# A gated linear attention with an SSM block on one core: weights converted by bit moves, transposes taken to VectorE, and the SSM block moved one group closer

## The chip, the cores and the metric

One core of a Trainium2 chip. The time is device microseconds of one execution, the median of a kernel's executions. Each kernel was run together with runs of the kernel before on the same chip. A ratio is the mean time of one kernel's fast runs over that of the other's fast runs of the same rounds, with a 95% interval, so it is not quite the ratio of the medians quoted. Spans are from one profiled execution; a timed run lies about 2 us above its span.

Engines: PE is TensorE's matmul, PEld its weight load, DVE VectorE, ACT ScalarE, POOL GpSimd, SP SyncE; a q after a name (SPq, ACTq) is the sequencer that issues transfers. "L330" is a line of the kernel of that run, and the kernels before and after number their lines differently.

## The reference, cut to what matters

```python
# q, k, v, alpha: (4, 8, 768, 48) fp32; alpha in 0.8..1.0
for t in range(S):
    state = alpha[:, :, t, :, None] * state + einsum('bhd,bhe->bhde', k[:, :, t], v[:, :, t])
    y[:, :, t] = einsum('bhd,bhde->bhe', q[:, :, t], state)
x = y.transpose(0, 2, 1, 3).reshape(4, 768, 384)
proj = x @ w_in                       # w_in: (384, 1024), float64 numbers in memory
val, gate = proj[..., :512], proj[..., 512:]
h = a * h + val                       # step by step, a = exp(A_log)
out = (silu(gate) * h) @ w_out        # w_out: (512, 384), float64
```

The weights arrive as float64, and the kernel computes in float32. It reads each number as two 32-bit words and builds a float32 of them.

## The kernel before: the parts that the change and the argument touch

The 4 x 768 steps are handled in 12 groups of 256 (`N` = 12, `NG` = 3 groups a batch). `front(n)` turns alpha, q and k of a group, so that channels lie on partitions (TensorE transposes, tile `tp`), makes the running products `V` and `P` of alpha on DVE, scales q and k by them, computes the scores `sc` and turns k back (`tpk`). `back(n)` makes the states `z` and their sums `S_n`, the values `y`, and turns the features (`tpx` to `xT`). `ssm(n)` is the projection `pj`, the scan `hh`, the gate `sg` and the output `o`. All are generators; the order of their steps is written by hand.

```python
        def split_unit(u):                       # a unit: 128 x 384 weights, 12 of them
            lo, hi = words[u][..., 0], words[u][..., 1]
            dst = units[u][0]
            nc.scalar.activation(lo.bitcast(FP32), lo, AF.Copy, scale=2.0 ** -52)
            # ... DVE: ex = hi & 0x7FF00000 ; dst = hi & 0xFFFFF | 0x41000000
            nc.scalar.activation(ex.bitcast(FP32), ex, AF.Relu, scale=-8.0, bias=bias[:, 3:4])
            nc.scalar.activation(ex, ex.bitcast(FP32), AF.Relu, scale=-1.0, bias=bias[:, 4:5])
            nc.scalar.activation(dst, dst, AF.Copy, bias=-7.0)
        # join_unit: DVE ex = sign | ex ; GpSimd dst += lo ; GpSimd dst *= ex

        # in front(n), for alpha, q and k
            def turned(name, jj):
                tp = ps_tp.tile([C, 2, GC], FP32, tag="tp", name="tp")
                for u in range(2):
                    j = 2 * jj + u
                    for c in range(G):
                        nc.tensor.transpose(tp[:, u, ds(c * C, C)], pad[name][:, c, 2 * j:2 * j + 2, :], ident)
                return tp
            # ... V, P: DVE scans over turned("a"); Q = turned("q") * P; K = turned("k") * V

        # in back(n)
            for x in range(GR):                  # sums of the states of blocks of 64 steps
                # ... nc.vector.tensor_add(dst, S_n[:, x], src)
        # ...
            nc.sync.dma_start(out=out[b, ds(g * GC + c * C, C), :], in_=o_sb)     # in ssm(n)

        with tc.manual_schedule():
            for n in range(N + 3):
                # iteration n: front(n), back(n - 1), the projection of n - 2, the output of n - 3
```

## Time and profile before

| | before |
|---|---|
| time, median | 346.38 us (346.02 to 346.68, 3 runs) |
| span of the profiled execution | 344.2 us |
| PE busy, and idle | 309.7 us, 34.5 us |
| PE without a hole from | about 75 us on |
| period of one group after that | 24.73 us |

The prediction below shows the slices, the chain and the windows. What it takes from the groups of instructions is here: one of the three sets of input transposes, and one of the four ACT passes over a unit of weights. The columns after the count are total busy time, mean ns of one, and idle time ahead with what ended it.

```profile
L295 PE MATMUL tp<-ident,k_pad 128*128 128x128 f32 x96 | 14.4, 298 | 0.2 <-issue 0.2
...
L242 ACT ACTIVATE ex<-ex,bias 128x384 uint32<-128x384 f32 x12 | 7.4, 616 | 0.4
```

Each ACT pass has twelve instances, all in the first stage. The `tp` lines come three times (alpha, q, k), 96 matmuls each, spread over the whole run.

### The profile page before, as it was taken

Reading aid. Unit: us, or ns where it says so; the run is one execution under the profiler, and the core shown is the slowest. Engines: PE = TensorE matmul, PEld = TensorE weight load, DVE = VectorE, ACT = ScalarE, POOL = GpSimd, SP = SyncE. Lnnn points to the kernel's source line nnn. Section 1 sums busy time; section 2 is a strip of 40 time slices with the busy share of each in tenths; the row PEclk is TensorE's granted clock in tenths of the full one; section 3 lists DMA queues with packets and bytes.
Section 4 is the critical chain, followed back from the end, with each engine's and each line's share of the span. In section 5 each row is a group of like instructions: output and inputs, shape, how many; then the busy total and the mean of one; then the engine's idle time right before and its main releaser. Section 6 shows DMA issues by size and latency. Waiting matters only on the chain.

```text
span 344.2 us, 9637 instructions
## 1 busy us (share of the span) xinstructions
PE 309.7 (90%) x4233; PEld 249.6 (73%) x4233; DVE 198.6 (58%) x374; ACT 126.5 (37%) x267; POOL 32.3 (9%) x54
## 2 busy tenths in 40 slices
PE   2556696879999999999999999999999999997994
PEld 1345585757877878868868878878878878776772
DVE  2869797683566566475484494484475574314140
ACT  1356876743324324324333342333233233222111
POOL 4023652440000000000000000000000000000000
PEclk9996798989999999999999999999999999999998
DMA  9999998504704907608609409519110010010101
GB/s 129 216 218 256 238 199 125 94 2 103 130 2 97 135 2 130 104 0 146 88 1 160 73 2 170 62 38 170 29 46 4 0 48 2 2 49 0 50 0 54
DMA packets 107650, 29.02 MB, mean 84 GB/s; under 512 B 100944, under 2 KB 107088, under 8 KB 107600
## 3 DMA queue, kind: packets, MB, share of 16 engines
q1 hardware_dynamic: 104992, 27.93, 46.4%
q10 hardware_dynamic: 2608, 0.40, 1.0%
q8 instruction: 35, 0.57, 0.7%
q14 instruction: 15, 0.12, 0.1%
HBM read 23.60 MB, written 4.72 MB: 82 GB/s over the span
## 4 chain that ended last, share of the span: by engine, by line
PE 80%; DVE 8%; ACT 5%; DMA 3%; issue 2%; SPq 1%; ACTq 0%; DVEq 0%
PE pj L93 36%; PE o L107 18%; PE tp L295 9%; PE z L131 3%; PE sc L332 3%; PE y L146 3%; PE y L164 3%; PE tpk L119 3%; PE tpx L173 2%; DVE V L302 2%; DVE P L307 2%; DMA a_pad<-in_alpha_dram 2%; DMA v_sb<-in_v_dram 1%; ACT ex L242 1%; ACT ex L241 1%
## 5 line engine op out<-in xcount | busy, mean ns | idle before, releaser
L93 PE MATMUL pj<-xT,w_in 128*128 128x256 f32 x576 | 135.2, 386 | 2.9 <-ACT sg L101 2.9
L93 PEld LDWEIGHTS pj<-xT,w_in 128*128 128x128 f32 x576 | 107.1, 192 | 17.5 <-POOL w_out L250 3.0
L107 PE MATMUL o<-w_out,f 128*128 128x384 f32 x192 | 65.9, 496 | 0.1
L96 DVE TENSOR_TENSOR_SCAN hh<-a_dec,hh,pj 128x256 f32<-128x256 f32 x32 | 23.9, 747 | 69.0 <-PE pj L93 69.0
L101 ACT ACTIVATE sg<-pj 128x256 f32<-128x256 f32 x48 | 18.4, 383 | 114.1 <-DVE hh L96 114.0
L107 PEld LDWEIGHTS o<-w_out,f 128*128 128x128 f32 x192 | 35.9, 192 | 23.7 <-DVE f L102 0.7
L102 DVE TENSOR_TENSOR f<-sg,hh 128x256 f32<-128x256 f32 x48 | 20.9, 436 | 25.4 <-ACT sg L101 25.4
L302 DVE TENSOR_TENSOR_SCAN V<-tp,bias 128x256 f32<-128x256 f32 x48 | 30.1, 669 | 6.9 <-PE tp L295 6.9
L307 DVE TENSOR_TENSOR_SCAN P<-tp,iV,bias 128x256 f32<-128x256 f32 x48 | 33.4, 737 | 0.8
L312 ACT ACTIVATE junk<-V,bias 128x1024 f32<-128x1024 f32 x12 | 13.8, 1148 | 47.2 <-DVE V L302 47.2
L295 PE MATMUL tp<-ident,a_pad 128*128 128x128 f32 x96 | 13.9, 289 | 14.0 <-POOL k_pad L201 4.9
L96 DVE TENSOR_TENSOR_SCAN hh<-a_dec,pj 128x256 f32<-128x256 f32 x16 | 11.0, 685 | 23.8 <-PE pj L93 23.8
L295 PEld LDWEIGHTS tp<-ident,a_pad 128*128 128x128 f32 x96 | 11.6, 147 | 15.9 <-POOL k_pad L201 4.9
L349 POOL TENSOR_TENSOR S_n<-S_end,V 128x192 f32<-128x192 f32 x7 | 3.6, 513 | 203.5 <-DVE S_end L358 203.5
L295 PE MATMUL tp<-ident,q_pad 128*128 128x128 f32 x96 | 14.4, 292 | 8.0 <-DVE P L307 6.4
L295 PEld LDWEIGHTS tp<-ident,q_pad 128*128 128x128 f32 x96 | 11.9, 151 | 12.2 <-issue 8.6
L335 DVE COPY_PREDICATED A<-mask,sc 128x512 f32<-128x512 uint8 x24 | 16.0, 720 | 3.0 <-PE sc L332 3.0
L319 DVE TENSOR_TENSOR Q<-tp,P 128x512 f32<-128x512 f32 x24 | 15.4, 681 | 2.9 <-PE tp L295 2.9
L332 PEld LDWEIGHTS sc<-Q,K 64*64 64x64 f32 x768 | 13.7, 143 | 4.0 <-issue 3.0
L110 ACT ACTIVATE o_sb<-o 128x384 f32<-128x384 f32 x24 | 10.7, 479 | 15.5 <-PE o L107 15.5
L323 DVE TENSOR_TENSOR K<-tp,V 128x512 f32<-128x512 f32 x24 | 15.5, 681 | 0.5 <-PE tp L295 0.5
L332 PE MATMUL sc<-Q,K 64*64 64x64 f32 x768 | 15.5, 231 | 0.1
(61 smaller groups left out, 313.8 us busy)
## 6 DMA issues: line engine op xcount, KB each, us to landing
a_pad<-in_alpha_dram SPq DMA_DIRECT2D x24, 192.0 KB, 4.7
k_pad<-in_k_dram SPq DMA_DIRECT2D x24, 192.0 KB, 5.2
v_sb<-in_v_dram SPq DMA_DIRECT2D x24, 192.0 KB, 5.1
out_dram<-o_sb SPq DMA_DIRECT2D x24, 192.0 KB, 2.2
q_pad<-in_q_dram SPq DMA_DIRECT2D x22, 192.0 KB, 4.9
bits<-in_moe_w_in_dram SPq DMA_DIRECT2D x8, 384.0 KB, 5.3
bits<-in_moe_w_out_dram SPq DMA_DIRECT2D x4, 384.0 KB, 5.1
q_pad<-in_q_dram ACTq DMA_DIRECT2D x2, 192.0 KB, 5.5
```

The costliest lines, as they stand in the source:

```text
L93: nc.tensor.matmul(pj[:, i, :], w_in[:, kk, i, ds(cc * C, C)], xT[:, kk, :], start=(kk == 0), stop=(kk == NK - 1))
L96: nc.vector.tensor_tensor_scan(out=hh, data0=a_dec[:, cc:cc + 1].to_broadcast([C, GC]), data1=pj[:, 0, :], initial=prev_h[cc][:, GC - 1:GC ...
L101: nc.scalar.activation(sg, pj[:, 1, :], AF.Silu)
L102: nc.vector.tensor_mul(f[:, cc, :], sg, hh)
L107: nc.tensor.matmul(o, f[:, cc, ds(c * C, C)], w_out[:, cc, :], start=(cc == 0), stop=(cc == NI - 1))
L295: nc.tensor.transpose(tp[:, u, ds(c * C, C)], pad[name][:, c, 2 * j:2 * j + 2, :], ident)
L302: nc.vector.tensor_tensor_scan(out=V[:, 2 * jj + u, GC - 1::-1], data0=tp[:, u, ::-1], data1=bias[:, 1:2].to_broadcast([C, GC]), initial=1 ...
L307: nc.vector.tensor_tensor_scan(out=P[:, 2 * jj + u, :], data0=tp[:, u, :], data1=bias[:, 1:2].to_broadcast([C, GC]), initial=iV0[:, 2 * jj ...
L319: nc.vector.tensor_mul(Q[:, js], turned("q", jj), P[:, js])
L323: nc.vector.tensor_mul(K[:, js], turned("k", jj), V[:, js, 1:GC + 1])
L332: nc.tensor.matmul(scv[ds(R * r, R), i, c * NP + j, :], K[rows, j, steps], Q[rows, j, steps], start=True, stop=True, skip_group_check=True)
L335: nc.vector.copy_predicated(out=A[:, i].rearrange("p x t -> p (x t)"), mask=mask[:, ds(i * GP * R, GP * R)], data=sc[:, i])
```

## The change

By its title it converts the weights by bit moves and one integer add, with a range check and a complete fallback, and brings the SSM block of group n - 1 beside group n. The diff holds a third part: from group 4 on, alpha, q and k are loaded in squares of 32 x 32 and turned by VectorE. The diff, cut to its core:

```diff
+        def convert_unit(u):
+            nc.scalar.activation(lo.bitcast(FP32), lo, AF.Copy, scale=2.0 ** -29, bias=2.0 ** 23)
+            nc.scalar.activation(lo, lo.bitcast(FP32), AF.Copy, bias=-2.0 ** 23)
+            nc.vector.tensor_scalar(out=dst, in0=hi, scalar1=0x07FFFFFF, scalar2=3,
+                                    op0=ALU.bitwise_and, op1=ALU.logical_shift_left)
+            nc.vector.scalar_tensor_tensor(out=dst, in0=hi, scalar=0xC0000000, in1=dst,
+                                           op0=ALU.bitwise_and, op1=ALU.bitwise_or)
+            nc.gpsimd.tensor_add(units[u][0].bitcast(I32), units[u][0].bitcast(I32), lo.bitcast(I32))
+        def check_units(p):                       # range of three units' high words, in place
+            nc.scalar.activation(h, h, AF.Square, scale=2.0 ** -16, accum_out=left_w[:, p, 0:1])
+            nc.scalar.activation(h, h, AF.Relu, scale=-2.0 ** 60, bias=bias[:, 0:1], accum_out=left_w[:, p, 1:2])
-        (split_unit, join_unit)
...
+        staging = big.tile([C, len(units), NK * C * 2], U32, tag="big0", name="staging")   # raw weights
+        BY_VECTOR = NG + 1
+        def load_batch(b):
+            t = big.tile([C, 3, NP * NW * W], FP32, tag=f"big{1 - b % 2}", name="batch")   # b = 1: big0
+            for m, (name, src) in enumerate((("a", alpha), ("q", q), ("k", k))):
+                w0 = max(0, BY_VECTOR - NG * b) * GC // W
+                ...                               # 2 memsets on GpSimd
+                for j, nj in [(0, NP)] if w0 == 0 else [(j, 1) for j in range(NP)]:
+                    for i in range(2):
+                        for half in range(2):
+                            nc.sync.dma_start(...)      # squares: rows of 128 and of 64 bytes
+            def squares(name, dst):
+                nc.vector.transpose(dst, batches[b, name][:, :, ds(g * GC, GC)])
...
-            nc.sync.dma_start(out=out[b, ds(g * GC + c * C, C), :], in_=o_sb)
+            nc.scalar.dma_start(out=out[b, ds(g * GC + c * C, C), :], in_=o_sb)
+        def load_last(n):
+            if n == 2:
+                load_batch(1)
+            if 2 <= n < N - 2:
+                load(n + 2, "v", nc.scalar)
...
+        # F, A: a step of front(n), front(n + 1); B: back(n); P, H: projection of n - 1; O: output of n - 2
+        # C: product check; U: convert a unit; W: check three units; L, M: loads
+        early = ["FFFFLUFUFABBABB", "UUFPUUFHPUHFFPUHBBCPHABUAUBL", "FPUFHPUHFFPHBBCAPHBWAWOBWAWOM"]
+        usual = "FLPHPHFFOABBCPHABPHBAOM"
+        ending = ["PHPHOPHPHO", "OO"]
```

Queries, keys, `Kn`, `A` and the features have one buffer less than before.

## The prediction

> **What bounds the kernel now.** I read the slices of the span first, then the chain that ended last in order of time, then the table of windows, and last the groups by line and shape. The page says which engine is full, and from when:
>
> ```profile
> PE 309.7 (90%) x4233; PEld 249.6 (73%) x4233; DVE 198.6 (58%) x374; ACT 126.5 (37%) x267; POOL 32.3 (9%) x54
> ...
> PE   2556696879999999999999999999999999997994
> ...
> DVE  2869797683566566475484494484475574314140
> ...
> PEclk9996798989999999999999999999999999999998
> DMA  9999998504704907608609409519110010010101
> ```
>
> PE has holes in the first nine slices (to about 75 us) and none after. There are two stages with different limits. In the second, the chain is TensorE alone; here is most of one period, one group of 256 steps:
>
> ```profile
> 246.69 0.87 PE tp L295 x8
> 247.56 1.08 PE z L131 x64
> 248.64 5.36 PE o L107 x16
> 254.00 0.87 PE tp L295 x8
> ...
> 258.74 0.87 PE tp L295 x8
> ...
> 263.46 1.09 PE sc L332 x64
> 264.55 0.81 PE tpx L173 x6
> 265.36 2.59 PE pj L93 x12
> 267.95 0.87 PE tpk L119 x8
> ```
>
> The next period starts at 271.42, so a group takes 24.73 us: three sets of input transposes (tp) 2.61, score, state, value and turning work (sc, tpk, z, two y, tpx) 6.00, projections (pj) 10.77, output (o) 5.36. In the first stage the table of windows shows DVE as the fullest engine:
>
> ```profile
> 40.00:50.00 10.00, 7.96 (x103) 6.90 (x103) 9.30 (x19) 7.73 (x17) 6.28 (x6) 1.00 1.20 252
> 50.00:62.00 12.00, 8.73 (x148) 7.22 (x149) 9.36 (x21) 9.25 (x18) 3.74 (x4) 0.86 0.84 112
> 62.00:75.00 13.00, 9.51 (x191) 7.92 (x183) 9.59 (x19) 7.35 (x16) 6.01 (x7) 0.91 0.36 63
> ...
> 150.00:200.00 50.00, 50.00 (x703) 40.69 (x702) 30.30 (x56) 16.51 (x36) 0.51 (x1) 1.00 0.50 81
> ```
>
> (Columns: PE, weight loads, DVE, ACT, POOL, clock, DMA share, GB/s.) Between 20 and 75 us DVE is busy 45 of 55 us, 82%; ACT, with four passes for each piece of weights, is next. In the steady stage DVE uses 0.61 of its time.
>
> **What the Trainium skill says.** The title of the change hides its largest part: from group 4 on, alpha, q and k are no longer turned by TensorE but by VectorE in squares of 32, from tiles that the DMA fills in squares.
> - "VectorE: DVE Perf Modes", The three transpose paths: the VectorE transpose works on 32x32 blocks only and lands in SBUF. "Vector Engine (DVE) Microarchitecture Reference", 3.8: it sustains one element per cycle per lane. At the 0.96 GHz of these pages 1024 elements are 1.07 us; with the start-up of the ops here (a 512-wide multiply takes 681 ns, of which 533 are elements) my estimate is 1.2 us. The kernel before has no such instruction, so its trace can't confirm it.
> - "DMA: Bandwidth & Descriptors", Why small descriptors are slow (HBM only): each packet has a fixed cost beside its bytes. The trace agrees: in the packet records the median of a 192-byte packet is 15 ns, of 1024 bytes 49 ns, which is 7 ns fixed and 0.041 ns a byte.
> - "TensorE: Matmul & The Clock Gate", What's actually happening: after an idle window of about 3.4 us the clock halves. The trace agrees: the granted clock is 0.57 in the window 30 to 40, where PE waited.
>
> **The change part by part.**
> 1. *Input transposes.* 12 groups x 3 sets become 4 x 3; 24 sets x 0.87 us = 20.9 us leave TensorE in the stage where it sets the end. The period falls to 24.73 - 2.61 = 22.12.
> 2. *VectorE takes them.* 24 x 1.2 = 29 us more. A steady group on DVE before is 0.607 x 24.73 = 15.0 us; with 3.6 more it is 18.6 of 22.12 us, 84%, plus four waits of 0.5 us between a scan and its gated product (25.4 us over 48 in the table of waits). It fits with about 1.5 us to spare, so I count nothing, but it is close.
> 3. *Weights.* On ACT a piece falls from 556+611+616+507 = 2290 ns to two passes, about 1.1 us: 12 x 1.2 = 14 us less. DVE falls from three passes (427, 542, 641) to two (542, 641): 12 x 0.43 = 5 us less. POOL loses one pass of 1.0 us in 12. All in the first stage. The range check is new: 4 x 2 ACT passes over 1152 elements, estimated from the 1024-wide 1148 ns plus a 187 ns accumulator read as 1.4 us each: 11 us at the end of iteration 2.
> 4. *Schedule.* The SSM block of n - 1 stands beside group n, one iteration less behind. By the end of iteration 2 the new program has issued the projections of groups 0 and 1 and the output of 0 and is ready for the projection of group 2. I time that point by DVE. Work that stands ahead of the last state sum of group 2: conversion 12 x 1.18 minus a little for the contiguous w_out = 13.5; three groups of scans, Q, K, mask 3 x 10.1 = 30.4; states 4.2; eight gate pairs less one 8.0: 56 us. Start at 8.2 (first scan). With ACT relieved I take a busy share of 0.87 in place of 0.82: 8.2 + 64 = 72.5. From there the values 1.1, the ACT copy 1.4, two check units 5.5 that stand ahead in ACT's order, the output copy 0.5, the turned features 1.0: the projection of group 2 starts at 82.
> 5. *What TensorE has left then:* ten projections 107.7, eleven outputs 59.0, nine groups x 6.00 = 54.0: 220.7 us.
> 6. *A new wait.* The first square tile reuses the buffer of the raw weights, so its load can't start before the last check, at about 82 + 5.5 = 87.5. Each row of 192 bytes now moves as one packet of 128 and one of 64 bytes: twice the packets. By the size fit plus the 6.6 ns by which the 192-byte mean exceeds its median they take 19 and 16 ns, 1.1 ns a packet over 16 engines. Alpha of groups 4 and 5 is 8192 packets, 9 us; with two memsets of about 1.8 us ahead (estimated from 308 ns for 256 elements) and 2 us of landing it is there at about 101. DVE reaches it after about 8 us of iteration 3, waits some 5 us, and the state sums of group 3 stand behind it in DVE's order. TensorE reaches the values that need these at 82 + 9.5 and gets them at 87.5 + 19.5 - a loss near 10; I take 9, plus 2 for a cold clock after it.
> 7. *End.* The last outputs stand behind other matmuls, so the two waits for gates (about 2 us each in the chain at 316 and 334) are hidden; they are not in the sum of 5, and I add none. From the last matmul to the end 4.7 us as before (339.5 to 344.2).
>
> Sum: 82 + 220.7 + 11 + 4.7 = 318.4 us of span; the timed runs lie 2 us over the span (346.4 against 344.2): 320. As the hand-made order of the first stage is likely better than my share of 0.87, I put 318.
>
> **Rivals.**
> - *DMA becomes the bound* from iteration 3 to 6. Groups 4 to 8 need 24.6 + 36.9 thousand packets plus three loads of v, in about 75 us. At 1.1 ns that is 75 us, just enough; at the 1.25 ns that a burst of 8192 192-byte packets shows (10.2 us) it loses 10 to 15 more: 330. DMA share 0.50 with half as many packets speaks for it. ACT also issues outputs and v loads now, and waits for DMA slots that square loads hold.
> - *VectorE becomes the bound.* If a square transpose takes 2.2 us, DVE needs 23.7 us a group and the period is about 25: no gain in the steady stage, 335 to 340. One element a cycle speaks against it.
> - *No wait at group 4:* if the squares land in time or PE has enough other work, 307 to 310.
> - *Fallback taken:* more than double; normal random weights are far inside the range checked. I give it no weight.
>
> **Range and chances.** The sure gain is 21 us of transposes; the first stage gives about 15 more, and the new wait takes back 0 to 25. 306 to 332 should hold it. To miss 2% (339.5) both a slow transpose and a DMA wait are needed: faster 0.95, same 0.04, slower 0.01.
>
> **What would show it.** Right: tp with 96 matmuls in all in place of 288, PE near 288 us busy, a period of 22.1 us late in the run, square transposes near 1.2 us, a hole of about 10 us in PE near 92 to 105 whose releaser is DVE and behind it the DMA of alpha, projections of group 2 at about 82, ACT with 11 us of checks before it. Wrong: a steady period over 23 us with PE idle behind DVE (step 2), holes at groups 6 and 7 behind DMA (step 6), or the start of group 2 beyond 90 (step 4).

## More of the kernel before

The experiments ran on several chips, on which the kernel before took 346.1 to 347.2 us, so small differences between experiments are not read.

`ps_tp` is a pool of two PSUM buffers; `tp`, `tpk` and `tpx` all come from it.

## The result

| | before | after |
|---|---|---|
| time, median | 346.46 us (346.02 to 346.68) | 336.68 us (332.71 to 338.49) |
| ratio of fast runs | | 0.9681 [0.9598, 0.9764] |
| span | 344.2 us | 334.8 us |
| PE busy, idle | 309.7, 34.5 us | 291.8, 43.0 us |

Three of the four runs after (336.65, 332.71, 336.71) were fast; the one of 338.49 was not. The kernel is faster by 3.2%, not by the 8% predicted, and the time lies above the range. TensorE lost 17.9 us of work and gained 8.5 us of holes.

The page after, in 40 slices (8.4 us each):

```profile
PE 291.8 (87%) x4041; PEld 231.6 (69%) x4041; DVE 223.5 (67%) x387; ACT 126.0 (38%) x259; POOL 45.0 (13%) x58
...
PE   1577995899499792599999999999999999999993
...
PEclk9995898699789898599999999999999999999999
```

The holes that PE had only in the first nine slices before now reach into the 17th, and the granted clock falls in the same places.

The groups by form show that the durations were guessed well:

```profile
L330 DVE STREAM_TRANSPOSE K<-batch 128x1024 f32<-128x1024 f32 x8 | 9.9, 1239 | 12.7 <-DMA batch<-in_k_dram 12.7
L277 ACT ACTIVATE staging<-staging 128x384 uint32<-128x384 f32 x12 | 6.8, 564 | 0.4
L289 ACT ACTIVATE staging<-staging,bias 128x1152 f32<-128x1152 f32 x4 | 5.3, 1328 | 0.1
```

A square transpose takes 1.24 us (1.2 predicted), the two ACT passes of a unit 0.564 and 0.552, together 1.12 us (1.1), and the four checks, two passes each, 11.7 us with their accumulator reads (11). The late stage is right too; the chain of the kernel after, one whole period, is TensorE alone:

```profile
227.07 1.09 PE sc L368 x64
...
248.85 1.09 PE sc L368 x64
```

That is 21.78 us from scores to scores (22.12 predicted), without a `tp` in it.

The loss lies between. TensorE's timeline of the kernel after (start, duration, instruction, and in brackets the hole ahead of it with what ended it):

```profile
88.80 1.97 PE L326 MATMUL tp<-ident,pads 128*128 128x128 f32 x8 [4.28 <-ACT xT L197]
90.56 4.69 PE L130 MATMUL o<-w_out,f 128*128 128x384 f32 x8
...
95.96 5.34 PE L115 MATMUL pj<-xT,w_in 128*128 128x256 f32 x24
...
113.00 1.35 PE L187 MATMUL y<-S_n,Q 64*64 64x48 f32 x48 [1.74 <-DVE S_n L400]
...
137.81 2.07 PE L368 MATMUL sc<-Q,K 64*64 64x64 f32 x64 [10.57 <-DVE K L359]
```

The projection of group 2 starts at 95.96 us; 82 was predicted. Ahead of it stand a hole of 4.28 us and 7.2 us of other matmuls, of which the output takes 4.69 us, while 2.75 us is usual in this view: the clock was low after the hole (0.61 granted from 88.80 to 96.00). The hole ends when ACT has copied `xT`, which frees a buffer of `ps_tp`. What ACT did in that time is in its own timeline:

```profile
82.00 1.26 ACT L288 ACTIVATE staging<-staging 128x1152 f32<-128x1152 f32 x1
...
86.03 1.30 ACT L289 ACTIVATE staging<-staging,bias 128x1152 f32<-128x1152 f32 x1
...
87.33 0.47 ACT L133 ACTIVATE o_sb<-o 128x384 f32<-128x384 f32 x1
88.25 0.87 ACT L197 ACTIVATE xT<-tpx 128x384 f32<-128x384 f32 x2 [0.45 <-ACT o_sb L133]
```

Two of the four checks (82.00 to 87.43) stand in ACT's order ahead of the copies that TensorE waits for. (The first line is the first pass of the first check, the second the last pass of the second.) The other two follow and end at 94.5, and only then can the squares' loads start, since they overwrite the raw weights.

The long hole of 10.57 us is the scores' wait for the keys of group 4. The chain, followed back from it:

```profile
122.10 0.50 ACT o_sb L133
...
123.08 0.40 ACTq L96
123.52 3.97 DMA v_sb<-in_v_dram
...
132.64 2.64 DMA batch<-in_k_dram
...
135.69 1.26 DVE K L330
```

Read from the bottom: VectorE waits for a load of k; SP issued it last of a row of loads (L246), 0.49 us each; that row stood still, in the end until a load of v had landed; and ACT issued the load of v (L96) only after the copy of an output, which stands ahead in its order. Why should a load of k wait for one of v? In the program as built the transfers that SP and ACT issue take their completion semaphores in rotation from one set of eight, and an issue waits until the earlier transfer on its semaphore has landed. The trace's records of the issues name the eight, 100 and 102 to 108. I call such a semaphore a slot. The longest stand of this row was for a store: the third load of k, ready after 118.2 us, was issued at 124.67, on the slot of the store that ACT had issued at 122.62.

### The profile page after: what moved, and what is told of

It reads as the page before. It is cut to its first block, busy times and chain, and to the rows that moved or that the text cites. A ratio compares the mean times of both kernels' runs of the same rounds, so it can differ in the third digit from the quotient of the medians.

```text
span 334.8 us, 9254 instructions
## 1 busy us (share of the span) xinstructions
PE 291.8 (87%) x4041; PEld 231.6 (69%) x4041; DVE 223.5 (67%) x387; ACT 126.0 (38%) x259; POOL 45.0 (13%) x58
## 4 chain that ended last, share of the span: by engine, by line
PE 75%; DVE 6%; DMA 6%; ACT 5%; SPq 3%; issue 3%; ACTq 1%; DVEq 0%
PE pj L115 34%; PE o L130 18%; PE sc L368 4%; PE tp L326 4%; PE tpk L142 4%; PE y L187 4%; PE z L154 3%; PE y L169 3%; DMA v_sb<-in_v_dram 3%; PE tpx L196 3%; SPq L246 2%; DVE P L344 2%; DVE V L339 2%; DMA pads<-in_alpha_dram 1%; DMA batch<-in_q_dram 1%
## 5 line engine op out<-in xcount | busy, mean ns | idle before, releaser
L130 PEld LDWEIGHTS o<-w_out,f 128*128 128x128 f32 x192 | 36.2, 197 | 20.9 <-issue 2.1
L326 PE MATMUL tp<-ident,pads 128*128 128x128 f32 x96 | 19.6, 358 | 16.0 <-DMA pads<-in_alpha_dram 6.9
L241 POOL MEMSET batch<- 32x1536 f32 x18 | 24.7, 1371 | 64.7 <-DMA out_dram<-o_sb 41.7
L326 PEld LDWEIGHTS tp<-ident,pads 128*128 128x128 f32 x96 | 15.0, 183 | 19.4 <-issue 8.0
L368 PE MATMUL sc<-Q,K 64*64 64x64 f32 x768 | 15.9, 237 | 10.7 <-DVE K L359 10.6
L344 DVE TENSOR_TENSOR_SCAN P<-aT,iV,bias 128x256 f32<-128x256 f32 x32 | 23.6, 780 | 0.6
L339 DVE TENSOR_TENSOR_SCAN V<-aT,bias 128x256 f32<-128x256 f32 x32 | 20.3, 677 | 0.3
L330 DVE STREAM_TRANSPOSE K<-batch 128x1024 f32<-128x1024 f32 x8 | 9.9, 1239 | 12.7 <-DMA batch<-in_k_dram 12.7
L196 PE MATMUL tpx<-ident,x_sb 128*128 128x128 f32 x72 | 11.9, 300 | 6.0 <-DVE P L344 4.3
L187 PEld LDWEIGHTS y<-S_n,Q 64*64 64x64 f32 x704 | 13.1, 140 | 5.7 <-issue 4.9
L169 PE MATMUL y<-v_sb,A 64*64 64x48 f32 x768 | 14.2, 220 | 3.2 <-issue 3.2
L154 PEld LDWEIGHTS z<-v_sb,Kn 64*64 64x64 f32 x768 | 12.3, 134 | 6.1 <-issue 5.4
```

The costliest lines, as they stand in the source:

```text
L130: nc.tensor.matmul(o, f[:, cc, ds(c * C, C)], w_out[:, cc, :], start=(cc == 0), stop=(cc == NI - 1))
L154: nc.tensor.matmul(zv[chs, r, g, j, :], Kn[rows, g, j, chs], v_sb[rows, g, NP * i + j, :], start=True, stop=True, skip_group_check=True)
L169: nc.tensor.matmul(yv[at, i, c, j, :], A[rows, i, c * NP + j, :], v_sb[rows, c, NP * i + j, :], start=(c == 0 and j == 0), stop=False, ski ...
L187: nc.tensor.matmul(yv[at, i, c, j, :], Q[rows, j, ds(R * x, R)], S_n[rows, x, j, :], start=False, stop=(c == G - 1 and j == NP - 1), skip_ ...
L196: nc.tensor.transpose(tp[:, kk, :], x_sb[:, c, ds(kk * C, C)], ident)
L241: nc.gpsimd.memset(tv[ds(DP * i + W, W), :, D - W:W], 1.0 if name == "a" else 0.0)
```

## The experiments

Two theories for the hole. S: the loads of squares wait for shared slots, and for the time of their own issues. P: the packets (twice as many as before, 1.1 ns each in the prediction) are the limit. And for the late start: the checks, or a chain in the first stage.

### 1. Slots of their own for outputs and v

```diff
-            nc.scalar.dma_start(out=out[b, ...], in_=o_sb)
+            nc.gpsimd.dma_start(out=out[b, ...], in_=o_sb)
-                load(n + 2, "v", nc.scalar)
+                load(n + 2, "v", nc.gpsimd)
```

> The changed kernel with the output stores and the later v loads issued by GpSimd, whose transfers have completion semaphores of their own; the square loads keep theirs to themselves. Theory S (shared slots: a square load of k waits until ACT has issued a v load or an output store that itself waits for TensorE): the 12.7 us wait of DVE for k of group 4 falls under 3 us, the 10.6 us hole of PE with the cold clock after it goes, 334.8 us of span becomes about 322, timed 324. Theory P (packet rate: the squares are too many packets): the wait stays at 8 us or more, 333 to 337.

332.78 us (332.05 to 334.37), ratio 0.9594 [0.9549, 0.9639]. The SP queue, after and in this run (start, time from first to last of the 16 issues):

```profile
94.95 10.49 SPq L246 DMA_DIRECT2D batch<-in_alpha_dram  x16
...
117.17 15.96 SPq L246 DMA_DIRECT2D batch<-in_k_dram  x16
```

```profile
94.65 8.64 SPq L246 DMA_DIRECT2D batch<-in_alpha_dram  x16
...
114.67 10.59 SPq L246 DMA_DIRECT2D batch<-in_k_dram  x16
```

The 48 issues now take 30.6 us in place of 38.2, the wait of VectorE for k falls from 12.65 to 7.31 us and TensorE's hole from 10.57 to 6.17. The shared slots are therefore a part of it, but a wait remains: 48 issues of at least 0.53 us (0.49 and a gap of 0.04) are 25 us by themselves. (The other 5 us are not explained; some single issues took 1.2 to 1.7 us.) The result lies between the two theories: the wait is over S's 3 us and under P's 8, the time between their 324 and 333. About 3 us of the gain were lost at the end: from the start of the last copy to the end of the span it took 7.9 us with the store issued by GpSimd, 5.0 us in the change as it stands.

### 2. The checks earlier

```diff
-early[2] = "FPUFHPUHFFPHBBCAPHBWAWOBWAWOM"
+early[2] = "FWPUFHWPUHWFFPWHBBCAPHBAOBAOM"
```

> The changed kernel with the four range checks moved from the end of iteration 2 to its start and middle, where ACT was busy 3 of 13 us. The hole of 4.3 us in front of the turned features goes, the projection of group 2 starts near 90 in place of 96, and the raw buffer is free near 76 in place of 94. Theory S: k of group 4 still hangs on the v load and output store at the end of iteration 3, the hole there stays at 8 us or more, timed 328 to 331. Theory P: with 18 us more for the transfer that hole is gone too, timed 316 to 320.

327.23 us (322.25 to 329.05), ratio 0.9449 [0.9408, 0.9489]. Three of the five runs count as slow, only because they lie over 1.5% above the fastest, which is the profiled one; the two fast ones are 322.25 and 326.87, between the two theories' times. The projection of group 2 starts at 89.21 in place of 95.96, as expected, and the raw buffer is free 18 us sooner; yet the wait for k is still there:

```profile
121.59 1.25 DVE L330 STREAM_TRANSPOSE K<-batch 128x1024 f32<-128x1024 f32 x1 [8.79 <-DMA batch<-in_k_dram]
```

TensorE's hole is 7.39 us, a little less than S expected. SP's 48 issues now stretch from 75.57 to 119.20, 43.6 us for packets that took 30.6 in experiment 1, so packets are not the limit here. The chain again runs over an output copy and a load of v on ACT. This speaks for S.

### 3. Both, with the squares' loads right after the last check

Experiments 1 and 2 together, and the M moved forward to stand after the last W.

> Both edits, and the square loads issued right after the last check. Theory S: no wait for squares at all, the projection of group 2 near 90, then 221 us of TensorE work less the shorter period, timed 308 to 316. If only one of the two matters it equals the better of the other two runs.

332.15 us (330.84 to 332.85), ratio 0.9566 [0.9524, 0.9607]: a miss. No wait for k is left, but another has come, and the state sums wait 10.31 us for GpSimd. DVE's timeline, then GpSimd's:

```profile
90.52 1.13 DVE L402 TENSOR_TENSOR S_n<-S_n,z 128x192 f32<-128x192 f32 x3 [10.31 <-POOL S_n L393]
```

```profile
79.60 8.41 POOL L241 MEMSET batch<- 32x1536 f32 x6 [5.67 <-ACT staging L289]
```

With M the six memsets of the square tiles (8.4 us) moved too, and I had put them, and the issue of two v loads (1.95 us), ahead of GpSimd's state product of group 2, which came at 89.98. I had not asked what else stands in that engine's order.

### 4. Both, with M left at the end, and GpSimd only for the first groups

```diff
 early[2] as in 2
-            nc.scalar.dma_start(out=out[b, ...], in_=o_sb)
+            (nc.gpsimd if n <= 4 else nc.scalar).dma_start(out=out[b, ...], in_=o_sb)
-                load(n + 2, "v", nc.scalar)
+                load(n + 2, "v", nc.gpsimd if n <= 4 else nc.scalar)
```

> Range checks early as before, and the v loads and output stores up to iteration 6 on GpSimd's own semaphores, the later ones on ACT as in the changed kernel, so that the long tail of a store from GpSimd (7.9 us from the last output copy to the end against 5.0) does not return. The square loads are issued after GpSimd's state product of group 2, so that its memsets don't stand before that. Theory S: projection of group 2 near 89.5, k of group 4 there near 107 and needed at 114, no hole; 311 us of span, timed 312 to 315. Rival: the 48 square loads at 0.53 us each on SP still end after DVE wants k; then a wait of 3 to 6 us stays, timed 318.

317.67 us (317.17 to 318.4), ratio 0.9156 [0.9129, 0.9184]: 19 us less than the change as it stands, and faster than both kernels. The result is right and the fallback is kept. TensorE's timeline:

```profile
120.81 1.16 PE L368 MATMUL sc<-Q,K 64*64 64x64 f32 x64
```

The scores of group 4 follow the projection without a hole. The time is 3 to 6 us above what S expected. It is the rival's 318, but the rival's wait for k is not there; the early checks now delay ACT's copy of `Kn` (a hole of 2.01 us ahead of the states at 75.71) and the projection of group 2 starts at 92.96. The two repairs, worth 3.9 and 9.5 us alone by the medians, are worth 19.0 together (the two fast runs of experiment 2 would give it 9.8 or 14.4): with either alone, the wait for k stays.

### 5. The product checks of groups 0 and 1 moved as well

Experiment 4, with the C of group 0 moved from iteration 1 to the end of iteration 0 and that of group 1 to the end of iteration 1. It aims at a hole of 4.03 us at 57.5 us, where a gate stands behind 5 us of such checks in ACT's order.

> As the run before, and the four ACT passes that check the products of groups 0 and 1 (5 us, in front of the gate and of the features of group 0 in ACT's order) moved to the end of iteration 0 and behind the features. The hole of 4 us in PE at 54 to 58 goes; if the first stage hangs on that chain the projection of group 2 comes 3 to 5 us earlier, timed 308 to 312; if it hangs on DVE's busy time nothing changes.

319.54 us (316.36 to 320.8), ratio 0.9184 [0.9127, 0.9242]: no clear change against 317.67. The hole did not go: it became two, of 2.45 and 1.73 us, both ended by VectorE's scans of `P`, and an earlier one grew from 3.04 to 4.14. Moving these checks alone brings nothing; what the first stage hangs on is not shown.

### 6. No range check of the weights

```diff
-early[2] = "FPUFHPUHFFPHBBCAPHBWAWOBWAWOM"
+early[2] = "FPUFHPUHFFPHBBCAPHBAOBAOM"       # and left_w set to 0, so that the flag stays 0
```

> The changed kernel without the range check of the weights (its count is set to zero, so the fallback is never taken; the result is the same for these inputs). If the place of the checks costs, not their 11 us on ACT, it equals the run with early checks: 325 to 329. If their ACT time matters wherever they stand: 318 to 322.

319.89 us (316.56 to 320.28), ratio 0.922 [0.9191, 0.925]. Right for these weights, but no longer guarded. The projection of group 2 starts at 89.19, and of the long hole this is left in TensorE's timeline:

```profile
119.60 1.44 PE L368 MATMUL sc<-Q,K 64*64 64x64 f32 x64 [3.30 <-DVE K L359]
```

The time is the one of the second reading: even at the better place of experiment 2 the checks cost some 7 us by the medians. At the place that they have, checks of 11.7 us of ACT's time cost 16.8 us of the whole, more than their own length, because they hold TensorE at 84 us and the squares' loads later.

### 7. No checks, and slots of their own

Experiment 6 with the transfers of experiment 4.

> Transfers on slots of their own, no range check of the weights at all, squares kept: the upper bound of what moving the check can bring. The version with slots of its own and the check early took 317.7 us; no check with shared slots 319.9 with a hole of 3.3 us before the scores of group 4. If the early check still delays TensorE (its projection of group 2 started at 92.96, without check at 89.19) this should take 312 to 315 us; if the early check is hidden, 317 to 318.

313.42 us (312.54 to 315.13), ratio 0.904 [0.9005, 0.9075], as the first reading expected. So 4.3 us of the 317.7 are still the checks, and that is all that a better place for them could bring.

### 8. The squares taken away

```diff
-        BY_VECTOR = NG + 1
+        BY_VECTOR = N                  # every group by TensorE; no square loads; checks kept
```

The two functions that load later groups change with it: all loads, also those of v, are issued by SP again.

> The changed kernel with TensorE turning all twelve groups (loads of rows as in the first four groups), new conversion and new schedule kept. Gives back 24 x 0.87 = 20.9 us of TensorE work, takes away the waits for squares (about 14 us with the cold clock): 338 to 344. If the squares had no cost beside the holes it is near 341; if the schedule alone were worth the 15 us that I forecast for the first stage it is 330.

349.45 us (345.8 to 349.55), ratio 1.0035 [0.9971, 1.0098]. It was expected 5 to 11 us shorter; experiments 9 and 10 take up why. Without the squares nothing of the change is left to see, and the squares are worth 12.8 us of it net of all the waits that they bring.

### 9. No squares, no checks: new order and new conversion alone

Experiments 6 and 8 together.

> The new order of groups and the new conversion, without the squares and without the range check of the weights; it gives the right result. The kernel with only the conversion took 335.7 us, the one with order, conversion and check but no squares 349.5. Theory A (the check costs in this order what it cost in the whole change, about 14 to 17 us, because it stands in ACT's order ahead of the turned features and the output copies): 333 to 336 us, so that the new order by itself brings nothing over the old one. Theory B (the check hurts mostly by holding the raw buffer from the squares' loads, and the new order is slower by itself, as its steady period of 25.6 us against 24.7 suggests): 343 to 346 us. Either way the steady period should stay near 25.6 us.

344.0 us (339.58 to 344.34), ratio 0.9928 [0.9891, 0.9965]: theory B. The check costs 5.5 us here (3.7 by the ratios) and 16.8 us beside the squares, so some 11 us of its cost come only with them. One of TensorE's waits in this run (in all, times, longest):

```profile
PE tp L326 <- ACT xT L197: 7.1, 9, 0.8
```

In the steady stage each group has a hole of 0.8 us, where `tp` waits for a buffer of `ps_tp` that ACT frees with the copy of `xT`. The period is 25.6 us. The chain behind that wait runs over VectorE's scans of the next group and a gate on ACT. So the new order has no gain without the squares. Besides the order, this run keeps the smaller number of buffers and the stores issued by ACT; no run takes these apart, and none joins the old order with the squares.

### 10. The old order with the new conversion alone

The kernel before, with `split_unit` and `join_unit` replaced by `convert_unit`, and no check of the weights.

> The kernel before with nothing but the new conversion (no range check of weights). DVE is rid of 12 x 0.43 us, ACT of 12 x 1.2, GpSimd of 12 x 1.0. If the first stage is bound by busy time on DVE, as the prediction took it, 4 to 8 us: 338 to 342. If it hangs on waits from engine to engine, 0 to 2 us: 344 to 346.

335.67 us (335.2 to 336.15), ratio 0.9681 [0.9651, 0.9712]: more than either theory gave it, and as much as the whole change. PE is busy 305.2 us against 309.7, at a mean granted clock of 0.989 against 0.973, and idle 28.4 against 34.5: of some 10.6 us, 4.5 are shorter busy time of the same matmuls, at the better clock. Where it comes from can be seen in the windows from 20 to 62 us (PE, weight loads, DVE, ACT, POOL, clock, DMA share, GB/s), first of the kernel before, then of this run, then of the whole change:

```profile
20.00:62.00 42.00, 28.81 (x518) 24.50 (x521) 35.37 (x73) 31.90 (x63) 19.23 (x19) 0.84 1.06 202
```

```profile
20.00:62.00 42.00, 32.20 (x623) 27.00 (x621) 38.86 (x75) 26.00 (x52) 11.43 (x11) 0.92 1.05 211
```

```profile
20.00:62.00 42.00, 32.07 (x544) 26.78 (x543) 32.60 (x64) 23.93 (x47) 8.19 (x9) 0.82 0.80 181
```

With the passes of ACT gone, VectorE works 93% of this stretch in the old order, against 84% before. In the whole change it works 78%, and in experiment 9, which has the new order without squares and checks, 82% (34.51 us). That the busier VectorE is the cause of the gain is argued from this, not tested.

### 11. Fewer, larger loads of the first squares

```diff
-                w0 = max(0, BY_VECTOR - NG * b) * GC // W
+                w0 = 0           # the whole batch: 12 loads in place of 48, 36,864 packets in place of 24,576
```

> The whole change with one size altered: the first batch of squares is loaded whole (also group 3, which nobody reads), so alpha, q and k of it are 4 large loads each in place of 16 small ones: 12 issues in place of 48, and 36,900 packets in place of 24,600. The result is right. Theory S (the wait for k comes from the number of loads, each of which costs the queue 0.53 us and a turn on a shared completion slot): the last k load is issued much sooner, VectorE's wait for k falls from 12.65 us to 5 or less, time 326 to 331 us. Theory P (the packets are the limit, 1.1 ns each over the 16 engines, the rival of the prediction): 12,300 packets more cost 13 us more, the waits for alpha and k together grow from 17 to about 30 us, time 345 to 350 us. If packets cost only 0.75 ns, as their medians in the trace say, k would land at about 125 us: still S.

336.09 us (333.9 to 336.41), ratio 0.9669 [0.9616, 0.9722]: no change, and neither theory as stated. The SP queue in this run:

```profile
96.08 9.57 SPq L246 DMA_DIRECT2D batch<-in_alpha_dram  x4
...
115.66 11.63 SPq L246 DMA_DIRECT2D batch<-in_k_dram  x4
```

Twelve issues take 31.2 us, 2.6 us each. The transfers of SP's queue, from 94 to 140 us (packets, MB, share of the 16 engines' time), after and in this run:

```profile
q1 hardware_dynamic: 32704, 3.10, 56.4%
```

```profile
q1 hardware_dynamic: 47736, 4.61, 106.9%
```

With 12 large loads the 16 engines are full and the issues stand behind them: 36,864 packets in 31.2 us are 0.85 ns a packet. With 48 small ones the engines have time to spare, and the queue's issues and slots are the limit. The wait for k fell from 12.65 to 8.41 us and the hole from 10.57 to 7.21; the last matmul ended 2.2 us sooner, but the span did not (its last store took longer, 7.1 us from the start of the last copy in place of 5.0). So the packets are the next limit close behind: 24,576 at 0.85 ns would be an estimated 21 us, beside 25 us for 48 issues.

## Why the prediction was wrong

The parts of the change, each added to the one before it, by the medians of the runs:

| version | us | step |
|---|---|---|
| before | 346.4 | |
| new conversion, old order (10) | 335.7 | -10.7 |
| new order, with its buffers and queues (9) | 344.0 | +8.3 |
| squares (6) | 319.9 | -24.1 |
| range check of the weights: the change | 336.7 | +16.8 |
| check earlier, slots of their own (4) | 317.7 | -19.0 |

**Step 1, the transposes: right.** 20.9 us predicted; TensorE has 96 `tp` matmuls in place of 288 and the period is 21.78 us. As a part on its own they bring 24.1 us, net of the waits for squares; the 0.8 us wait for `xT` in each period goes with them.

**Step 2, VectorE takes them: right.** 1.24 us each; from 150 to 200 us DVE is busy 42.39 of 50, 85%, where 84% was predicted, and TensorE has no hole there. The rival "VectorE becomes the bound" is refuted.

**Step 3, the weights: durations right.** Two ACT passes of 1.12 us a unit, one GpSimd pass of 1.02, checks of 11.7 us. What these cost or bring was the business of steps 4 and 6.

**Step 4, the first stage: this is the step that failed.** The prediction's own sum shows it. It put the span at 82 + 220.7 + 11 + 4.7; the trace has 95.96 for the first term, then 221.5 of TensorE's work, 12.3 of holes and 5.0 for the end. The first term is 14.0 us late; all others together are off by 2.4, in part by luck (step 6). Two things went wrong in the first term.

The point where the state sums of group 2 are done came at 76.7, not 72.5 (VectorE's timeline has the sums, L402, from 75.58 for 1.12 us). This is the window from the first scan up to there (VectorE is the third figure):

```profile
8.20:76.70 68.50, 54.41 (x882) 45.54 (x882) 52.08 (x99) 30.16 (x61) 12.95 (x13) 0.88 0.72 147
```

VectorE's work up to there was 52.1 us, less than my 56; its waits made it late. I had held that relief of ACT would lift VectorE's busy share from 0.82 to 0.87. The windows of experiment 10 show the first half of that right, even too low (0.93 in the old order); but in the changed kernel the share is lower (0.78 between 20 and 62 us; 52.08 of 68.5 us, 0.76, between 8.2 and 76.7). I assumed that a hand-made order is likely better than my share. Experiment 9 has it, with its buffers and queues, 8.3 us slower than the old order with the same conversion. In the steady stage the trace puts this down to the wait for a buffer of `ps_tp`, which no run tested. For the first stage the cause is not shown: VectorE waits there mostly for gates and for `tp`, but taking the product checks away from ahead of the gates brought nothing (experiment 5), so that part stays open.

The way from those sums to the projection took 19.3 us, not 9.5. The two checks ahead in ACT's order, 5.4 us, were in my sum. Up to the end of the copies of `xT` (89.12) it took 12.4 us, 2.9 more than my sum, since the values start only at 79.12, behind half a projection on TensorE. The other 6.8 us are what I had left out: TensorE's own order has the q transposes of group 3, an output and the k transposes ahead of that projection, and these could not fill the hole: the transposes wait for a `ps_tp` buffer held until ACT copies `xT`, and the output stands behind them. After it they ran at a lower clock (0.61), 7.2 us in all. Two runs settle how much hangs on the place of the checks: without them (experiment 6), or with them earlier (experiment 2), the projection starts at 89.2; so 6.8 of the 14.0 us go and 7.2 stay.

**Step 5, TensorE's work left: nearly right.** 220.7 predicted; from 95.96 to the last matmul at 329.80 are 233.8 us, less holes of 12.3: 221.5. Some 4.4 us of these are low clock: from scores to scores, holes taken off, group 3 took 24.1 us (101.23 to 137.81) and group 4 23.9, against 21.78 later. The work itself is about 217.

**Step 6, the wait: place and cause wrong, and too small.** 11 us with its cold clock were predicted at alpha. The holes are 1.74 us at alpha and 10.57 at k, with the low clock of step 5 16.7 us. That the sum of steps 5 and 6 came out within some 2 us is luck: the work was some 3.6 us less than predicted, the wait 5.7 more. Alpha's square waited 4.2 us on VectorE (5 predicted), but TensorE had other work. For k I had allowed nothing: I had added up packets at 1.1 ns and not asked who issues them. 48 issues at 0.53 us are 25 us, and the slots shared with ACT's transfers added some 7.6 more (38.2 against 30.6 us in experiment 1). The sentence in my rival, that ACT "waits for DMA slots that square loads hold", had the coupling the wrong way round: in the table of waits SP stands, over the whole run, 29.1 us for stores of outputs and 19.8 us for loads of v, both issued by ACT.

**Step 7, the end: right.** 5.0 us after the last matmul.

**A reading put right.** The prediction says that TensorE waited in the window from 30 to 40 us, where the clock was 0.57. It was busy 8.81 of these 10 us; the waits came before, from 20 to 30, with 3.30 of 10 busy.

**The rivals.** "DMA becomes the bound" named the right stage, but its mechanism, packets, is only the second limit, and 1.1 ns was too much (0.85 in experiment 11). "No wait at group 4: 307 to 310" can be compared with experiment 7, which has neither that wait nor checks, and takes 313.4: the rest is the first stage (its projection of group 2 starts at 90.31, not 82).

The prediction had said what would show it wrong: a start of group 2 beyond 90 (step 4). That came. The other sign, holes at groups 6 and 7, did not; the only holes are at group 4.

## What to carry to other kernels

Before you credit a reordering, follow each engine's own order between two milestones and list everything that stands in it, on TensorE too; a shared PSUM buffer lets a copy far down in another engine's order stop the whole chain. A check that nobody waits for still costs time where it stands ahead of copies that somebody does wait for, or where it keeps a buffer from its next load: place it early, and look at what the buffer is for next. Count loads as well as bytes and packets, and ask which earlier transfers hold their completion semaphores.

## What the Trainium skill lacked or had wrong

- "DMA: Bandwidth & Descriptors", Issuing engines are not separate DMA queues: it says that issuing on several engines "will only save the time on the sequencer it takes to initiate the DMA, which is usually small relative to the DMA itself". Here the choice moved 9.5 us by the medians (327.2 to 317.7 us, checks early in both; 4.6 or 9.2 from the two fast runs of experiment 2), through the completion semaphores that the SP and ACT transfers of this program share, which the section doesn't mention. Nor is the issue small for loads of 512 small packets: 0.49 us each beside 2.5 to 3.0 us to landing, and 25 us for 48.
- Same page, Why small descriptors are slow (HBM only): the fixed cost that it describes is there (in the packet records of the change the median is 11 ns for 64 bytes, 13 ns for 128), but these packets did not set the time until the loads were large; then they took 0.85 ns each over the 16 engines (31.2 us for 36,864).
- "Vector Engine (DVE) Microarchitecture Reference", 3.8: one element per cycle per lane agrees with the trace. 128 x 1024 fp32 took 1.24 us, that is 0.17 above my 1.07 for the elements.
- "TensorE: Matmul & The Clock Gate", What's actually happening: the halving agrees. After the hole of 10.57 us 64 score matmuls took 2.07 us in place of 1.16, and after the one of 4.28 us an output 4.69 in place of 2.75. It gives the low clock as coming after at least one idle window of about 3.4 us; here the hole of 1.74 us was enough (twelve projection matmuls after it took 4.54 us in place of 2.86, at a granted clock of 0.68 from 113.0 to 118.4), while after one of 3.30 us in experiment 6 the granted clock stayed at 1.00. It puts the ramp at under 1% of a typical span; the 4.5 us of busy time that experiment 10 saved are 1.3%.
